# Two heads' keys and values on alternating partitions, in a one-token decode layer

## The chip, the cores and the metric

The kernel runs on one core of one Trainium2 chip. Its time is the device time of one execution in microseconds (us); the metric is the median of several executions. The profile is one further execution, recorded by the hardware profiler. The engines are named as in the profile: PE (TensorE, matrix products), PEld (its weight loads), DVE (VectorE), ACT (ScalarE), POOL (GpSimd) and SP (SyncE, which here only issues transfers). PSUM is the memory that matrix products write.

## The reference

One token `x` of 1024 numbers passes a layer norm. The result goes two ways, and both come back to `x`:

```
xn  = layernorm(x)                                  # 1 x 1024
q   = xn @ wq                                       # 32 heads of 128
k,v = the last 4096 rows of the cache, 4 key heads  # query head h uses key head h // 8
p   = softmax(q k^T / sqrt(128));  o = p v
out = x + o @ wo + (gelu(xn @ w_gate) * (xn @ w_up)) @ w_down
```

All of it is float32. The layer reads wq and wo (16.78 MB each), 4 heads of keys and 4 of values (2.10 MB each, 16.78 MB in all), and w_gate, w_up and w_down (14.68 MB each): 94.38 MB, each byte once, for a product with one row.

## The kernel before, in words

Everything that is read passes through one buffer, `ring`, of 128 partitions with 32768 numbers each. The table `PLAN` (L39) names the loads in order, the column at which each is put, and the older load whose place it takes. `load` (L105) issues a load's transfers on SP's queue, which works in order: SP stops at a transfer until the last reader of that part of the ring has finished, and everything later waits behind it. The order is wq in two halves (`q` 0 and 1), the keys and values of heads 0 and 1 (`k` 0, `v` 0), half of w_gate, the keys and values of heads 2 and 3 (`k` 1, `v` 1), the other half of w_gate, then w_up, wo and w_down.

A head's window is 4096 rows of 128 numbers. `window` (L76) gives each of 128 partitions 32 rows in a run, 16 KB. The two heads of a pair lie side by side in the ring, 4096 columns each; `half` (L440) is the column at which the second begins.

Products with one row are split between PE and DVE. `project` (L227) gives the even rows of a load to PE, which writes to `acc`, and the odd rows to DVE, which adds them up by partition in `part` (`add_scaled`, L207). `projected` (L240) then lets PE sum `part` over the partitions, and adds that to `acc`. `contract` (L425) does the same for wo and w_down with `out_p` and `out_part`.

The main loop (L441) walks the plan in the loads' order, and each engine works in program order. For the keys of a pair (L445): `transpose_keys` (L265) turns 32 blocks of 128x128 on PE, four to a PSUM buffer `kt_p` of which there are two, and ACT copies each buffer to `kT`; for the first pair `projected("q")` and `queries` (L243) follow, in which ACT copies q's rows to `q_sb`, PE turns them and DVE puts them into `qz`; then `scores` (L275) multiplies `qz` with `kT` in eight products of 32 rows, 8 of which are the head's queries, DVE takes each row's maximum, and ACT takes the exponential and its sum. The second head's transposes and scores follow. `values` (L291) turns the probabilities `p`, copies them (`pT`), and multiplies with the values in 32 products into `o_p`.

Each of the four head groups g has four row blocks with a maximum and a sum of their own. `maxima`, `factors` and `normalizers` (L319 to L344) bring them to a common maximum and turn the sums into `weight`; `heads` (L346) scales `o_p`, adds the blocks with the matrix `pick` and spreads the result over `oz`, which wo's product uses. These four stand between the loads of w_gate and w_up.

Of the kernel before, what the change touches and what calls it, by code (L numbers as in the profile page):

```python
# [33 lines left out]
SCALE = DH ** -0.5  # L34
GELU_C = math.sqrt(2.0 / math.pi)
# [15 lines left out]
def tile_decode_layer(  # L51
# [24 lines left out]
    def window(cache, g):  # L76
        return cache[0, g, SK - WIN:, :].rearrange("(p j) d -> p j d", p=P)
# [67 lines left out]
    qz = consts.tile([P, HKV, 32], F32, name="qz")  # L145
# [17 lines left out]
    pick = consts.tile([P, 2, 2, REP, 8], F32, name="pick")  # L163
    nc.vector.memset(pick, 0.0)
    for odd in range(2):
        nc.vector.tensor_copy(
            pick[:, odd, odd], same[:, 0, 0:REP].unsqueeze(2).to_broadcast([P, REP, 8])
        )
# [6 lines left out]
    def layer_norm():  # L175
# [20 lines left out]
        nc.scalar.activation(st[:, 4:5], st[:, 3:4], AF.Sqrt)  # L196

# [45 lines left out]
    def queries():  # L243
        q_sb = work.tile([P, 2, NB], F32, name="q_sb", tag="rows")
        nc.scalar.activation(q_sb, acc["q"], AF.Copy)
        q_p = psum.tile([P, 2, 4, 4], F32, name="q_p", tag="tp", bufs=2)
        for b in range(2):
            for hh in range(4):
                nc.tensor.matmul(
                    q_p[:, b, hh, :], q_sb[:, b, hh * P:(hh + 1) * P], ident[:, 0:P:32],  # L250
                    start=True, stop=True,
                )
            nc.vector.tensor_copy(
                qz[:, 2 * b:2 * b + 2, 0:8].rearrange("p s (t h) -> p s t h", t=2),
                q_p[:, b].rearrange("p h (s t) -> p s t h", s=2),
            )


    m = work.tile([P, HKV], F32, name="m")
    negm = work.tile([P, HKV], F32, name="negm")  # L260
    l = work.tile([P, HKV], F32, name="l")
# [53 lines left out]
    top = work.tile([HKV, 4, 32], F32, name="top")  # L315
    weight = work.tile([P, HKV], F32, name="weight")
    sel = same.rearrange("p c h -> p (c h)")

    def maxima():  # L319
        mt_p = small("mt_p")  # L320
        nc.tensor.transpose(mt_p[:HKV, :P], m, ident)
        nc.vector.reduce_max(
            top[:, 0, :], mt_p[:HKV, :P].rearrange("g (c h) -> g h c", c=4), axis=AX.X
# [4 lines left out]
    def factors():  # L328
        mm_p = small("mm_p")
        nc.tensor.transpose(mm_p[:, :HKV], top.rearrange("g c h -> g (c h)"), ident[:HKV, :HKV])  # L330
        d = work.tile([P, HKV], F32, name="d")
        nc.vector.tensor_sub(d, m, mm_p[:, :HKV])
        e = work.tile([P, HKV], F32, name="e")
        nc.scalar.activation(e, d, AF.Exp, scale=SCALE)
        le = work.tile([P, HKV], F32, name="le")
        nc.vector.tensor_mul(le, l, e)
        return e, le

    def normalizers(e, le):
        ls_p = small("ls_p")  # L340
        nc.tensor.matmul(ls_p[:, :HKV], sel, le, start=True, stop=True)
        r = work.tile([P, HKV], F32, name="r")
        nc.vector.reciprocal(r, ls_p[:, :HKV])
        nc.vector.tensor_mul(weight, e, r)  # L344

    def heads():  # L346
        o_sb = work.tile([P, HKV, DH], F32, name="o_sb")
        for g in range(HKV):
            nc.vector.tensor_scalar(
                o_sb[:, g, :], o_p[:, g, :], weight[:, g:g + 1], None, op0=ALU.mult  # L350
            )
# [3 lines left out]
        for odd in range(2):  # L355
            nc.tensor.matmul(
                ot_p, pick[:, odd].rearrange("p o h s -> p (o h s)"),
                o_sb.rearrange("p (a o) d -> p o a d", o=2)[:, odd],
                start=odd == 0, stop=odd == 1,
            )  # L360
# [80 lines left out]
    for key, _, _ in PLAN:  # L441
# [68 lines left out]
```

## Time and profile before

| | |
|---|---|
| time, median of 3 runs | 229.37 us (229.12 to 229.40) |
| the profiled execution's own time | 229.1 us |
| its span, first to last instruction | 227.3 us |
| busy share of the span: PE, DVE, ACT | 53%, 43%, 15% |
| mean rate of the transfers | 416 GB/s |
| transfers' queue q1 | 3752 packets, 94.38 MB |

The span is what the profile's times count from. The busy shares are means over stages that differ: while keys and values are worked on, PE and ACT do most, and while the weights are, PE and DVE. A packet is what one of the 16 DMA engines moves at a time. The profile gives a queue's packet time as a share of 16 engines over the stretch asked for; packets that overlap on an engine can make that more than 100%. The granted clock is the share of TensorE's 2.4 GHz that it was given in a stretch; 0.50 is the level of 1.2 GHz.

### The profile page before, as it was taken

Reading aid. Unit: us, or ns where it says so; the run is one execution under the profiler, and the core shown is the slowest. Engines: PE = TensorE matmul, PEld = TensorE weight load, DVE = VectorE, ACT = ScalarE, POOL = GpSimd, SP = SyncE. Lnnn points to the kernel's source line nnn. Section 1 sums busy time; section 2 is a strip of 40 time slices with the busy share of each in tenths; the row PEclk is TensorE's granted clock in tenths of the full one; section 3 lists DMA queues with packets and bytes.
Section 4 is the critical chain, followed back from the end, with each engine's and each line's share of the span. In section 5 each row is a group of like instructions: output and inputs, shape, how many; then the busy total and the mean of one; then the engine's idle time right before and its main releaser. Section 6 shows DMA issues by size and latency. Waiting matters only on the chain.

```text
span 227.3 us, 2496 instructions
## 1 busy us (share of the span) xinstructions
PE 120.4 (53%) x1100; PEld 62.9 (28%) x1100; DVE 97.0 (43%) x105; ACT 33.1 (15%) x57; POOL 0.7 (0%) x6
## 2 busy tenths in 40 slices
PE   0120900687866888595745390255219906452754
PEld 0010200154453746364511010111004903121322
DVE  7030920690202091201149489158219606993600
ACT  2000000054174307453200310000000000000000
POOL 1000000000000000000000000000000000000000
PEclk9999975599679699978879978559956655875879
DMA  9899899799999799999999999999999999999991
GB/s 369 370 461 462 369 484 438 334 438 421 437 484 484 327 424 417 421 510 428 394 407 434 439 469 454 394 493 392 430 461 392 438 412 415 421 456 395 424 385 51
DMA packets 3774, 94.53 MB, mean 416 GB/s; under 512 B 426, under 2 KB 434, under 8 KB 1076
## 3 DMA queue, kind: packets, MB, share of 16 engines
q1 hardware_dynamic: 3752, 94.38, 97.0%
q8 instruction: 8, 0.13, 0.2%
q14 instruction: 2, 0.02, 0.0%
q10 hardware_dynamic: 12, 0.01, 0.0%
HBM read 94.38 MB, written 0.00 MB: 415 GB/s over the span
## 4 chain that ended last, share of the span: by engine, by line
DMA 79%; DVE 14%; PE 5%; issue 0%; SPq 0%; DVEq 0%
DMA ring<-in_B_w_gate 26%; DMA ring<-in_A_wq 18%; DMA ring<-in_A_wo 14%; DVE part L212 13%; DMA ring<-in_B_w_up 11%; DMA ring<-in_B_w_down 10%; PE out_p L421 5%; DVE part L210 1%; SPq L118 0%; DVE y L485 0%; DVEq L212 0%
## 5 line engine op out<-in xcount | busy, mean ns | idle before, releaser
L212 DVE SCALAR_TENSOR_TENSOR part<-ring,xz,part 128x3584 f32<-128x3584 f32 (+1 forms) x9 | 37.2, 4129 | 22.2 <-DMA ring<-in_A_wq 12.4
L271 PE MATMUL kt_p<-ident,ring 128*128 128x128 f32 x128 | 21.5, 327 | 7.0 <-ACT kT L272 6.3
L272 ACT ACTIVATE kT<-kt_p 128x512 f32<-128x512 f32 x32 | 17.8, 595 | 43.9 <-PE kt_p L271 43.9
L222 PE MATMUL acc_q<-ring,xz 128*32 128x512 f32 x64 | 11.1, 858 | 22.2 <-DMA ring<-in_A_wq 22.2
L212 DVE SCALAR_TENSOR_TENSOR out_part<-ring,oz,out_part 128x1024 f32<-128x1024 f32 x15 | 19.3, 1285 | 7.9 <-DMA ring<-in_A_wo 7.4
L421 PE MATMUL out_p<-ring,hz 128*32 128x256 f32 x160 | 14.5, 520 | 13.7 <-DMA ring<-in_B_w_down 13.7
L421 PE MATMUL out_p<-ring,oz 128*32 128x256 f32 x128 | 12.3, 569 | 17.0 <-DMA ring<-in_A_wo 17.0
L271 PEld LDWEIGHTS kt_p<-ident,ring 128*128 128x128 f32 x128 | 16.4, 163 | 15.2 <-ACT kT L272 9.6
L222 PE MATMUL acc_u<-ring,xz 128*32 128x512 f32 x56 | 10.8, 838 | 10.7 <-DMA ring<-in_B_w_up 7.0
L283 DVE TENSOR_REDUCE m<-s_p 128x1 f32<-128x1024 f32 x4 | 4.9, 1224 | 26.7 <-PE s_p L280 26.7
L210 DVE TENSOR_SCALAR part<-ring,xz 128x3584 f32<-128x3584 f32 (+1 forms) x3 | 6.5, 2172 | 14.8 <-DMA ring<-in_A_wq 7.4
L421 PEld LDWEIGHTS out_p<-ring,hz 128*32 128x32 f32 x160 | 6.7, 146 | 21.5 <-DMA ring<-in_B_w_down 12.3
L421 PEld LDWEIGHTS out_p<-ring,oz 128*32 128x32 f32 x128 | 5.5, 162 | 23.9 <-DMA ring<-in_A_wo 18.0
L308 PE MATMUL o_p<-ring,pT 128*32 128x128 f32 x256 | 9.5, 309 | 4.7 <-ACT pT L303 4.7
L212 DVE SCALAR_TENSOR_TENSOR out_part<-ring,hz,out_part 128x1024 f32<-128x1024 f32 x8 | 10.3, 1285 | 3.9 <-DMA ring<-in_B_w_down 3.6
L222 PE MATMUL acc_g<-ring,xz 128*32 128x512 f32 x56 | 8.9, 719 | 4.5 <-DMA ring<-in_B_w_gate 4.5
L222 PEld LDWEIGHTS acc_q<-ring,xz 128*32 128x32 f32 x64 | 2.6, 150 | 29.8 <-issue 15.8
L308 PEld LDWEIGHTS o_p<-ring,pT 128*32 128x32 f32 x256 | 8.0, 123 | 5.8 <-ACT pT L303 5.8
L280 PE MATMUL s_p<-kT,qz 128*32 128x512 f32 x64 | 8.4, 645 | 0.0
L222 PEld LDWEIGHTS acc_u<-ring,xz 128*32 128x32 f32 x56 | 2.1, 138 | 17.6 <-DMA ring<-in_B_w_up 7.7
L178 PE MATMUL xt_p<-ident,x_rows 2*128 2x2 f32 x4 | 0.6, 252 | 10.4 <-DMA x_rows<-in_A_x 10.4
L300 PE MATMUL pt_p<-ident,p 128*128 128x128 f32 x32 | 5.9, 347 | 0.0
(94 smaller groups left out, 76.8 us busy)
## 6 DMA issues: line engine op xcount, KB each, us to landing
ring<-in_B_w_gate SPq DMA_DIRECT2D x2, 7168.0 KB
ring<-in_A_k_cache SPq DMA_DIRECT2D x4, 2048.0 KB
ring<-in_A_v_cache SPq DMA_DIRECT2D x4, 2048.0 KB, 23.3
ring<-in_B_w_down SPq DMA_DIRECT2D x2, 4096.0 KB, 24.3
ring<-in_B_w_up SPq DMA_DIRECT2D x2, 3584.0 KB, 26.3
ring<-in_B_w_up SPq DMA_DIRECT2D x1, 7168.0 KB
ring<-in_B_w_down SPq DMA_DIRECT2D x2, 2048.0 KB, 23.8
ring<-in_B_w_down SPq DMA_DIRECT2D x3, 512.0 KB
```

Of the source, the lines that this page charges most:

```text
L178: nc.tensor.transpose(xt_p[:, r * NJ:(r + 1) * NJ], x_rows[:, r:NR * P:NR], ident[:NJ, :NJ])
L210: nc.vector.tensor_scalar(total, w, factor, None, op0=ALU.mult)
L212: nc.vector.scalar_tensor_tensor(total, w, factor, total, op0=ALU.mult, op1=ALU.add)
L222: nc.tensor.matmul(acc[kind][32 * c:32 * c + 32, b, :], z, w[:, n * NB:(n + 1) * NB], start=start, stop=stop,)
L271: nc.tensor.transpose(t_p[:, jj * P:(jj + 1) * P], kn[:, j * DH:(j + 1) * DH], ident)
L272: nc.scalar.activation(kT[:, i, :], t_p, AF.Copy)
L280: nc.tensor.matmul(s_p[32 * c:32 * c + 32, b, :], qz[:, g, :], kT[:, i, :], start=True, stop=True)
L283: nc.vector.reduce_max(m[:, g:g + 1], s_p, axis=AX.XY)
L300: nc.tensor.transpose(t_p[:, jj * P:(jj + 1) * P], p[:, b, jj * P:(jj + 1) * P], ident)
L308: nc.tensor.matmul(o_p[32 * c:32 * c + 32, g, :], pT[:, b, jj, 32 * c:32 * c + 32], vn[:, j * DH:(j + 1) * DH], start=(b == 0 and jj == 0) ...
L421: nc.tensor.matmul(out_p[32 * c:32 * c + 32, :], z, w[:, c * CO:(c + 1) * CO], start=start, stop=stop)
```

## The change

Two heads of a pair now share the ring's columns. `window` cuts a head into 64 runs of 64 rows, 32 KB each, and `load` writes the first head to the even and the second to the odd partitions, 8192 columns wide. So each half of the load holds half of both heads, and each of `transpose_keys`, `scores` and `values` works on half the rows of two heads at a time. `qz` carries both heads' queries, 16 of 32 rows, in one tile for each pair. In the scores every second column belongs to the other head; the maximum is taken for even and odd columns apart, `away` (0 or -1e30, by the row's head) rules one of them out, and the exponential of each is taken with a bias of its own. Two groups now hold two parts of the same heads, so the later steps join them by pairs.

Besides, `projected("q")` and the copy of q's rows come ahead of the first key transposes. A small exponential in the layer norm loads ACT's table there. DVE copies three (1, 4 and 6) of the eight buffers of transposed keys.

```diff
     def window(cache, g):
-        return cache[0, g, SK - WIN:, :].rearrange("(p j) d -> p j d", p=P)
+        return cache[0, g, SK - WIN:, :].rearrange("(p j) d -> p j d", p=P // 2)
...
+        if key[0] in "kv":
+            for odd, src in enumerate(sources(*key)):
+                dst = ring[odd:P:2, at:at + RING // 4]
+                nc.sync.dma_start(dst, src.rearrange("p j d -> p (j d)"))
+            loaded[key] = ring[:, at:at + RING // 4]
+            return
...
-    qz = consts.tile([P, HKV, 32], F32, name="qz")
+    qz = consts.tile([P, 2, 32], F32, name="qz")
...
+    away = consts.tile([P, 2], F32, name="away")
+    nc.vector.reduce_sum(away[:, 1:2], same[:, 0, REP:2 * REP], axis=AX.X)
+    nc.vector.tensor_scalar(away[:, 0:1], away[:, 1:2], -FAR, None, op0=ALU.mult)
+    nc.vector.tensor_scalar(away[:, 1:2], away[:, 1:2], FAR, -FAR, op0=ALU.mult, op1=ALU.add)
...
+        zero = work.tile([P, 1], F32, name="zero")
+        nc.scalar.activation(zero, unit[:, 1:2], AF.Exp)
...
-    def queries():
+    def query_rows():
         q_sb = work.tile([P, 2, NB], F32, name="q_sb", tag="rows")
         nc.scalar.activation(q_sb, acc["q"], AF.Copy)
+        return q_sb
+
+    def queries(q_sb):
...
-            nc.scalar.activation(kT[:, i, :], t_p, AF.Copy)
+            if i in (1, 4, 6):
+                nc.vector.tensor_copy(kT[:, i, :], t_p)
+            else:
+                nc.scalar.activation(kT[:, i, :], t_p, AF.Copy)
...
-                s_p[32 * c:32 * c + 32, b, :], qz[:, g, :], kT[:, i, :], start=True, stop=True
+                s_p[32 * c:32 * c + 32, b, :], qz[:, g // 2, :], kT[:, i, :], start=True, stop=True
             )
-        nc.vector.reduce_max(m[:, g:g + 1], s_p, axis=AX.XY)
-        nc.vector.tensor_scalar(negm[:, g:g + 1], m[:, g:g + 1], -SCALE, None, op0=ALU.mult)
+        s = s_p.rearrange("p b (n odd) -> p odd (b n)", odd=2)
+        m2 = work.tile([P, 2], F32, name="m2")
+        nc.vector.reduce_max(m2, s, axis=AX.X)
+        nc.vector.tensor_add(m2, m2, away)
+        nc.vector.reduce_max(m[:, g:g + 1], m2, axis=AX.X)
+        nc.vector.scalar_tensor_tensor(
+            bias[:, g, :], m[:, g:g + 1].to_broadcast([P, 2]), -SCALE, away, op0=ALU.mult, op1=ALU.add
+        )
         p = work.tile([P, 2, NB], F32, name="p", bufs=2)
-        nc.scalar.activation(
-            p, s_p, AF.Exp, bias=negm[:, g:g + 1], scale=SCALE, accum_out=l[:, g:g + 1]
-        )
+        for odd in range(2):
+            nc.scalar.activation(
+                p.rearrange("p b (n odd) -> p odd (b n)", odd=2)[:, odd], s[:, odd], AF.Exp,
+                bias=bias[:, g, odd:odd + 1], scale=SCALE, accum_out=l[:, g, odd:odd + 1],
+            )
...
     def heads():
...
-        for odd in range(2):
-            nc.tensor.matmul(
-                ot_p, pick[:, odd].rearrange("p o h s -> p (o h s)"),
-                o_sb.rearrange("p (a o) d -> p o a d", o=2)[:, odd],
-                start=odd == 0, stop=odd == 1,
-            )
+        nc.tensor.matmul(ot_p, pick.rearrange("p h s -> p (h s)"), o_sb, start=True, stop=True)
...
             kn = loaded.pop(key)
+            if i == 0:
+                projected("q", 8)
+                q_sb = query_rows()
             transpose_keys(2 * i, kn[:, :half])
             if i == 0:
-                projected("q", 8)
-                queries()
+                queries(q_sb)
```

Left out above: the maxima, factors and normalizers, which gain one reduce, one addition and broadcast operands, the head scaling (two multiplications and two multiply-adds for four multiplications), and the setup of `pick`.

PE's order around the first keys, before: the products with wq, then the first group of key transposes (`kt_p`), and only then the sum of DVE's part (`acc_q<-part`) and q's transposes (`q_p`).

```order
L222 MATMUL acc_q<-ring,xz 32x512 x32
L271 MATMUL kt_p<-ident,ring 128x128 x32
L222 MATMUL acc_q<-part,unit 32x512 x8
L249 MATMUL q_p<-ident,q_sb 128x4 x8
L280 MATMUL s_p<-kT,qz 32x512 x8
L271 MATMUL kt_p<-ident,ring 128x128 x32
```

The same place now:

```order
L235 MATMUL acc_q<-ring,xz 32x512 x32
L235 MATMUL acc_q<-part,unit 32x512 x8
L289 MATMUL kt_p<-ident,ring 128x128 x32
L265 MATMUL q_p<-ident,q_sb 128x4 x8
L301 MATMUL s_p<-kT,qz 32x512 x8
L289 MATMUL kt_p<-ident,ring 128x128 x32
```

The sum has moved ahead of the 32 transposes; the counts of products are the same.

SP's order with its waits, before, from the first keys to w_gate's second half (a name with _49 is a semaphore of that engine or DMA queue):

```order
L118 DMA ring<-in_A_k_cache 128x4096 [waits DMAHW1_49,PE_49]
L118 DMA ring<-in_A_k_cache 128x4096 [waits DMAHW0_49,DVE_49]
L118 DMA ring<-in_A_v_cache 128x4096 [waits PE_49]
L118 DMA ring<-in_A_v_cache 128x4096 [waits DMAHW2_49,DVE_49]
L118 DMA ring<-in_B_w_gate 128x14336 [waits DMAHW3_49,DMAHW6_49,DVE_49,PE_49]
L118 DMA ring<-in_A_k_cache 128x4096 [waits DMAHW7_49,DMAHW4_49,PE_49]
L118 DMA ring<-in_A_k_cache 128x4096 [waits DMAHW5_49,DMAHW0_49,PE_49]
L118 DMA ring<-in_A_v_cache 128x4096 [waits DMAHW1_49,PE_49]
L118 DMA ring<-in_A_v_cache 128x4096 [waits DMAHW2_49,PE_49]
L118 DMA ring<-in_B_w_gate 128x14336 [waits DMAHW3_49,DVE_49,PE_49]
```

The same loads now:

```order
L113 DMA ring<-in_A_k_cache 64x8192 [waits DMAHW1_49,DVE_49,PE_49]
L113 DMA ring<-in_A_k_cache 64x8192 [waits DMAHW0_49]
L113 DMA ring<-in_A_v_cache 64x8192 [waits DVE_49,PE_49]
L113 DMA ring<-in_A_v_cache 64x8192 [waits DMAHW2_49]
L125 DMA ring<-in_B_w_gate 128x14336 [waits DMAHW3_49,DMAHW6_49,DVE_49,PE_49]
L113 DMA ring<-in_A_k_cache 64x8192 [waits DMAHW7_49,DMAHW4_49,PE_49]
L113 DMA ring<-in_A_k_cache 64x8192 [waits DMAHW5_49,DMAHW0_49]
L113 DMA ring<-in_A_v_cache 64x8192 [waits DMAHW1_49,PE_49]
L113 DMA ring<-in_A_v_cache 64x8192 [waits DMAHW2_49]
L125 DMA ring<-in_B_w_gate 128x14336 [waits DMAHW3_49,DVE_49,PE_49]
```

The number of loads and their order are the same. The first load of each pair now carries the waits of both for PE and DVE, and the second follows it at once.

## Rows read from the trace of the kernel before

**Rows 1.** The page: the span, q1's share of 16 engines, the last chain's shares.
```profile
span 227.3 us, 2496 instructions
...
q1 hardware_dynamic: 3752, 94.38, 97.0%
...
DMA 79%; DVE 14%; PE 5%; issue 0%; SPq 0%; DVEq 0%
```

**Rows 2.** Windows: start:end length, busy us of each engine, PEclk, DMA share, GB/s.
```profile
0.00:2.00 2.00, 0.00 (x0) 0.00 (x0) 1.00 (x5) 0.00 (x0) 0.70 (x6) 1.00 0.89 296
...
97.70:223.00 125.30, 66.12 (x649) 32.50 (x652) 63.77 (x59) 8.22 (x15) 0.00 (x0) 0.73 0.99 423
223.00:227.30 4.30, 1.31 (x19) 0.38 (x8) 0.42 (x1) 0.00 (x0) 0.00 (x0) 1.00 0.01 3
```

**Rows 3.** Timeline from 215 us: start, busy, engine, line, operation, count [idle before].
```profile
218.53 5.78 PE L421 MATMUL out_p<-ring,hz 128*32 128x256 f32 x64 [2.54 <-DMA ring<-in_B_w_down]
```

**Rows 4.** DMA queue, 43 to 60 us: packets, MB, share of 16 engines.
```profile
q1 hardware_dynamic: 493, 7.29, 100.5%
```

**Rows 5.** The same, 80 to 97 us.
```profile
q1 hardware_dynamic: 491, 7.26, 100.8%
```

**Rows 6.** The same, 189 to 206 us.
```profile
q1 hardware_dynamic: 240, 7.34, 100.4%
```

**Rows 7.** Timeline of SP: start, time from first to last issue, transfers.
```profile
0.74 0.86 SPq L118 DMA_DIRECT2D ring<-in_A_wq  x2
...
28.86 1.05 SPq L118 DMA_DIRECT2D ring<-in_A_v_cache  x2
...
52.07 17.53 SPq L118 DMA_DIRECT2D ring<-in_A_k_cache  x2
77.24 4.10 SPq L118 DMA_DIRECT2D ring<-in_A_v_cache  x2
...
98.76 26.12 SPq L118 DMA_DIRECT2D ring<-in_B_w_up  x3
```

**Rows 8.** Timeline of PE, the first and second pair of heads.
```profile
41.89 5.04 PE L222 MATMUL acc_q<-ring,xz 128*32 128x512 f32 x32 [13.09 <-DMA ring<-in_A_wq]
46.86 1.09 PE L271 MATMUL kt_p<-ident,ring 128*128 128x128 f32 x8
...
51.97 1.92 PE L222 MATMUL acc_q<-part,unit 128*32 128x512 f32 x16
55.03 1.05 PE L249 MATMUL q_p<-ident,q_sb 128*128 128x4 f32 x8 [1.14 <-ACT q_sb L245]
...
57.34 2.63 PE L280 MATMUL s_p<-kT,qz 128*32 128x512 f32 x16
...
85.00 1.06 PE L271 MATMUL kt_p<-ident,ring 128*128 128x128 f32 x8 [0.63 <-DMA ring<-in_A_k_cache]
...
111.82 0.27 PE L321 MATMUL mt_p<-ident,m 128*4 128x128 f32 x1
```

**Rows 9.** Timeline of DVE: the last row of wq, w_gate's second half.
```profile
46.46 4.49 DVE L212 SCALAR_TENSOR_TENSOR part<-ring,xz,part 128x4096 f32<-128x4096 f32 x1
...
116.55 7.94 DVE L212 SCALAR_TENSOR_TENSOR part<-ring,xz,part 128x3584 f32<-128x3584 f32 x2 [3.77 <-DMA ring<-in_B_w_gate]
```

**Rows 10.** Groups by line: count | busy us, mean ns | idle before, releasers.
```profile
L283 DVE TENSOR_REDUCE m<-s_p 128x1 f32<-128x1024 f32 x4 | 4.9, 1224 | 26.7 <-PE s_p L280 26.7
...
L286 ACT ACTIVATE p<-s_p,negm 128x1024 f32<-128x1024 f32 x4 | 4.5, 1115 | 8.5 <-DVE negm L284 8.5
...
L286 ACT ACT_TABLE_LOAD x1 | 1.3, 1283 | 6.5 <-DVE negm L284 6.5
...
L245 ACT ACTIVATE q_sb<-acc_q 128x1024 f32<-128x1024 f32 x1 | 1.0, 1024 | 1.3 <-PE acc_q L222 1.3
...
L284 DVE TENSOR_SCALAR negm<-m 128x1 f32<-128x1 f32 x4 | 0.6, 153 | 0.1
```

**Rows 11.** Windows, the first two us after PE resumes with wq.
```profile
43.00:45.00 2.00, 2.00 (x12) 0.39 (x8) 2.00 (x1) 0.00 (x0) 0.00 (x0) 0.56 1.09 467
```

More of the change, by code (lines that the diff above doesn't have):

```diff
@@ L34 @@
 SCALE = DH ** -0.5
+FAR = 1e30
 GELU_C = math.sqrt(2.0 / math.pi)
@@ L160, in tile_decode_layer @@
         nc.vector.tensor_copy(same[:, c, :], same[:, 2, :])
-    pick = consts.tile([P, 2, 2, REP, 8], F32, name="pick")
-    nc.vector.memset(pick, 0.0)
-    for odd in range(2):
-        nc.vector.tensor_copy(
-            pick[:, odd, odd], same[:, 0, 0:REP].unsqueeze(2).to_broadcast([P, REP, 8])
-        )
+    pick = consts.tile([P, 2 * REP, 8], F32, name="pick")
+    nc.vector.tensor_copy(pick, same[:, 0, 0:2 * REP].unsqueeze(2).to_broadcast([P, 2 * REP, 8]))
     low = consts.tile([P, 8], F32, name="low")
     nc.vector.reduce_sum(low, ident.rearrange("p (h s) -> p s h", s=8), axis=AX.X)
+    away = consts.tile([P, 2], F32, name="away")
+    nc.vector.reduce_sum(away[:, 1:2], same[:, 0, REP:2 * REP], axis=AX.X)
+    nc.vector.tensor_scalar(away[:, 0:1], away[:, 1:2], -FAR, None, op0=ALU.mult)
+    nc.vector.tensor_scalar(away[:, 1:2], away[:, 1:2], FAR, -FAR, op0=ALU.mult, op1=ALU.add)
     def small(name):
@@ L253, in queries @@
             nc.vector.tensor_copy(
-                qz[:, 2 * b:2 * b + 2, 0:8].rearrange("p s (t h) -> p s t h", t=2),
+                qz[:, b, 0:16].rearrange("p (s t h) -> p s t h", s=2, t=2),
                 q_p[:, b].rearrange("p h (s t) -> p s t h", s=2),
@@ L259, in tile_decode_layer @@
     m = work.tile([P, HKV], F32, name="m")
-    negm = work.tile([P, HKV], F32, name="negm")
-    l = work.tile([P, HKV], F32, name="l")
+    bias = work.tile([P, HKV, 2], F32, name="bias")
+    l = work.tile([P, HKV, 2], F32, name="l")
     keys, probs = {}, {}
@@ L312, in values @@
                     )
-    top = work.tile([HKV, 4, 32], F32, name="top")
-    weight = work.tile([P, HKV], F32, name="weight")
+    top = work.tile([2, 4, 32], F32, name="top")
+    weight = work.tile([P, 2, 2], F32, name="weight")
     sel = same.rearrange("p c h -> p (c h)")
@@ L320, in maxima @@
         mt_p = small("mt_p")
-        nc.tensor.transpose(mt_p[:HKV, :P], m, ident)
+        for f in range(2):
+            nc.tensor.transpose(mt_p[:2, f * P:(f + 1) * P], m[:, f:HKV:2], ident)
         nc.vector.reduce_max(
-            top[:, 0, :], mt_p[:HKV, :P].rearrange("g (c h) -> g h c", c=4), axis=AX.X
+            top[:, 0, :], mt_p[:2, :2 * P].rearrange("g (c h) -> g h c", c=8), axis=AX.X
         )
@@ L329, in factors @@
         mm_p = small("mm_p")
[L330 to L333, printed above, removed]
+        nc.tensor.transpose(mm_p[:, :2], top.rearrange("g c h -> g (c h)"), ident[:2, :2])
+        d = work.tile([P, 2, 2], F32, name="d")
+        nc.vector.tensor_sub(
+            d, m.rearrange("p (g f) -> p g f", f=2), mm_p[:, :2].unsqueeze(2).to_broadcast([P, 2, 2])
+        )
+        e = work.tile([P, 2, 2], F32, name="e")
         nc.scalar.activation(e, d, AF.Exp, scale=SCALE)
         le = work.tile([P, HKV], F32, name="le")
-        nc.vector.tensor_mul(le, l, e)
+        nc.vector.tensor_add(le, l[:, :, 0], l[:, :, 1])
+        nc.vector.tensor_mul(le, le, e.rearrange("p g f -> p (g f)"))
         return e, le
@@ L341, in normalizers @@
         nc.tensor.matmul(ls_p[:, :HKV], sel, le, start=True, stop=True)
-        r = work.tile([P, HKV], F32, name="r")
-        nc.vector.reciprocal(r, ls_p[:, :HKV])
-        nc.vector.tensor_mul(weight, e, r)
+        r = work.tile([P, 2], F32, name="r")
+        nc.vector.reduce_sum(r, ls_p[:, :HKV].rearrange("p (g f) -> p g f", f=2), axis=AX.X)
+        nc.vector.reciprocal(r, r)
+        nc.vector.tensor_mul(weight, e, r.unsqueeze(2).to_broadcast([P, 2, 2]))
     def heads():
-        o_sb = work.tile([P, HKV, DH], F32, name="o_sb")
-        for g in range(HKV):
+        o_sb = work.tile([P, 2, DH], F32, name="o_sb")
+        for g in range(2):
             nc.vector.tensor_scalar(
-                o_sb[:, g, :], o_p[:, g, :], weight[:, g:g + 1], None, op0=ALU.mult
+                o_sb[:, g, :], o_p[:, 2 * g, :], weight[:, g, 0:1], None, op0=ALU.mult
+            )
+            nc.vector.scalar_tensor_tensor(
+                o_sb[:, g, :], o_p[:, 2 * g + 1, :], weight[:, g, 1:2], o_sb[:, g, :],
+                op0=ALU.mult, op1=ALU.add,
             )
         ot_p = psum.tile([P, 2, DH], F32, name="ot_p", tag="tp", bufs=2)
-        for odd in range(2):
-            nc.tensor.matmul(
-                ot_p, pick[:, odd].rearrange("p o h s -> p (o h s)"),
-                o_sb.rearrange("p (a o) d -> p o a d", o=2)[:, odd],
-                start=odd == 0, stop=odd == 1,
-            )
+        nc.tensor.matmul(ot_p, pick.rearrange("p h s -> p (h s)"), o_sb, start=True, stop=True)
         own = work.tile([P, 2, 8, WIDE], F32, name="own", tag="rows")
```

## The prediction

> **What bounds the kernel now.** I read the page's totals first [rows 1]. The queue that carries the weights and the cache (q1) is busy for 97.0% of the span with 94.38 MB, and the chain that ended last is 79% DMA, 14% DVE and 5% PE. The windows then say where the missing 3% is [rows 2]: between 97.7 and 223.0 us the DMA engines are busy 0.99 of the time, and after 223.0 nothing moves. So there is one uninterrupted stream from about 1 us to 223 us, and a tail: the last matmuls run to 224.3 us (218.53 + 5.78) [rows 3], then come one addition and the output. A change gains only what shortens that stream or that tail, and it loses whatever opens a hole in the stream. The tail is not touched.
>
> Next I read how the stream runs on the rows to be changed. In 43 to 60 us, inside the first keys and values, q1 has 493 packets, 7.29 MB, 100.5% of 16 engines [rows 4]; in 80 to 97 us, inside the second pair, 491 packets, 7.26 MB and 100.8% [rows 5]; in 189 to 206 us, inside w_down, whose first two loads bring 32 KB a partition, 240 packets, 7.34 MB and 100.4% [rows 6]. The first two are the layout of before (16 KB a partition), the third is the packet size that the change gives to keys and values.
>
> Last I read when SP can issue. Its waits don't hurt as long as each load is issued before the loads ahead of it have drained. The second pair's keys go out from 52.07 to 69.60 (52.07 + 17.53) and its values from 77.24 to 81.34 [rows 7].
>
> **The change part by part.**
>
> *Larger packets.* Engine time for each MB is share times 16 engines times 17 us over MB: 1.005 x 272 / 7.29 = 37.50 us [rows 4], 1.008 x 272 / 7.26 = 37.77 us [rows 5], and 1.004 x 272 / 7.34 = 37.21 us [rows 6]. Keys and values are 8 transfers of 2.10 MB, 16.78 MB. The mean of the first two less the third is 0.43 us, times 16.78 over 16 engines: 0.45 us of stream. By the rates of the same windows (MB over 17 us: 429 and 427 against 432 GB/s) it is 16.78/0.428 - 16.78/0.432 = 39.2 - 38.8 = 0.4 us. Lower end: none, if what slows these windows goes by bytes or by other traffic. Shares above 100% say that packets overlap a little, which hides part of a packet's fixed cost, so I take 0.35 us.
>
> *64 rows on every second partition.* No row shows a transfer that names 64 partitions. Below, it costs nothing, if the 16 engines share these rows as evenly as the 128. Above, if pairs of engines meet on one path, it takes twice the time, 39.2 us more. The nearest rows, rows 4 to 6, show all engines full with three different row counts, so I take zero and keep the other as a rival. The Trainium skill (SBUF — State Buffer, "Door 1: The DMA port swizzle") speaks against transfers to 64 partitions: neighbouring ones reach half of the 16 ports, and it gives 196 GB/s for them; by that rate the 16.78 MB would take 86 us, not 39. By the same section's formula every second partition from 0 to 126 reaches all 16 ports, which leaves the sum as it is; no row here shows either.
>
> *Waits of SP.* Before, each half of a load waited for the half of the ring that it overwrites; now both of a pair wait for the whole. For the first pair that costs nothing: before, the last of them was issued by 29.9 us [rows 7], and PE waits for wq's second half until 41.89 [rows 8]. For the second pair I work out when PE has done with the first.
> - Keys of pair 0: the first half is in use from 46.86 [rows 8], and the second is 2.10 MB / 0.430 = 4.9 us behind it, so all has landed by 51.8 us. PE now idles from 46.9 to 51.0, when DVE ends the last row of wq (46.46 + 4.49) [rows 9], and then sums q in 1.92 us. After the long wait before 41.89 PE ran at a granted clock of 0.56 in 43 to 45 us, so near 1.2 of 2.4 GHz [rows 11]; if the short one has the same effect the sum takes up to 3.8 us. Transposes start at 52.9 to 54.8 us.
> - Eight groups of transposes, with ACT's copies between them, took 46.86 to 51.97, 5.1 us, 0.64 for a group. DVE now copies three of eight. The trace has no such copy; DVE's 128x1024 reduce out of PSUM took 1.22 us [rows 10], so about 0.6 us for half as many elements: no faster than ACT. What two copiers gain lies between nothing and the waits between pairs of groups; the copy of q's rows, 1.02 us on ACT [rows 10], now stands ahead of the first of them and costs about as much. I leave 5.2 us.
> - q's transposes (55.03 to 57.34, 2.3 us) and the scores (2.63 us) follow [rows 8]: the first scores end at 63.0 to 64.9 us, where before they ended at 59.97.
> - From there to the issue of the second values it took 81.34 - 59.97 = 21.4 us. Off it goes the table load, 1.28 us [rows 10], which now stands in the layer norm, where ACT has little else. To it come, for each of two groups of scores, three small DVE steps in place of one at 0.15 us (0.3 us and the gaps, 0.45) and a second exponential: two of 512 elements for one of 1024 at 1.115 us add between nothing and 0.56 us [rows 10], I take 0.3. In all 21.4 - 1.3 + 1.5 = 21.6 us. The operands now take every second element; the lower end is no cost, and if it doubled the reduce (1.22 us) and the exponentials (1.1 us) they would cost 2 x 2.3 = 4.6 us more. I take none.
> - So the second values are issued by 84.6 to 86.5 us, 3 to 5 us later than now. They are needed when the second keys have drained. PE waited for the first half of these until 85.00, the other half is 2.10 / 0.428 = 4.9 us behind, so all have landed by 89.9, and the last packet is a little earlier: 87 to 89 us. From issue to first packets it takes at most 1.3 us: issued at 0.74 [rows 7], with 296 GB/s already in the window that ends at 2.0 [rows 2]. The limit is 86 to 87.5 us. I take no hole, but the cover is thin.
> - Queued behind these values on SP are w_gate's second half and all later loads, in order. The second keys now go out together when the second group of transposes ends, about 73 us where the later one went at 69.3; they are needed when w_gate's first half has drained, 4.19 MB (9.8 us) ahead of the second keys' end and so at 77 to 79 us, less the lead: near 76.
> - Pair 1: PE starts at 89.9 rather than 85.00 and needs about the 26.8 us it took to 111.8, so until 116.7. Behind that stands DVE's reduce of the maxima, and behind that, in order, DVE's work on w_gate, which began at 116.55 [rows 9]. The last w_up load waits for it (issued by 98.76 + 26.12 = 124.9 [rows 7]); 55.6 MB stand ahead of it, of which 0.6 has moved at 2.0 us, and at 430 GB/s it is needed at about 129. A slip of 3 us is covered.
>
> *The rest.* The constants lose a memset and gain three small DVE operations while wq's first half is still on its way. The factors, normalizers and heads gain and lose a few short operations while w_up streams, 14.68 MB or 34 us. Cost: zero, since no load waits on them with less than the slack above; without that cover, some three steps of 0.15 us, about 0.5 us.
>
> **The sum.** 229.1 us (span 227.3 [rows 1] and 1.8 around it) less 0.35 is 228.75 for an execution like the profiled one. That one lay 0.27 below the median of the runs shown; the same 0.35 off 229.37 gives 229.0 us.
>
> **The rivals.**
> *Late values.* A hole in front of the second values. For it: an issue at 84.6 to 86.5 against a limit of 86 to 87.5, and the two unknowns (clock, strided operands) both push one way. Against it: every other estimate in that chain is from rows at both clock levels. It decides from the moment the issue passes the limit, and each us beyond is a us of the stream. With the low clock and half of the doubled operands it is 86.5 + 2.3 = 88.8 against 86.7, the middle of the limit: 229.0 + 2.1 = 231.1 us; with all of the 4.6 us 233.4 us, with none of it 229.0. That is slower than before.
> *Two engines on one path.* Keys and values at half the rate: 229.4 + 39.2 = 268.6 us; if engines fall out of step, half of it, 249. For it: 64 rows is a count that no row shows. Against it: every second partition still spreads over the whole range, and the trace's rates don't fall for any row count seen.
> *The packets do not matter.* The engine cuts or overlaps so that the 0.35 us does not appear: 229.4 us, no change. For it: the stretch from 97.7 to 223.0 us moves 423 GB/s [rows 2], below either window of keys and values, with packets of many sizes in it, so other things than packet size set the rate too.
>
> **How the numbers follow.** The likeliest case, a slightly shorter stream with no hole, has 64%; its own range is 228.3 to 229.4. Its lower part would need fewer stray stalls as well as fewer packets. Late values have 17%, the shared path 7%, no effect of packets 12%. A difference under 0.2%, 0.46 us, is about what a measurement of this kernel cannot tell from no change. 0.35 us is under that: of the 64, 28 lie beyond it and 36 within. Faster 0.28; same 0.36 + 0.12 = 0.48; slower 0.17 + 0.07 = 0.24. The range reaches from 228.3 to 231.0: it leaves out the shared path and the longer half of the holes, and some 3% below.
>
> **What would show it.** In the changed profile the windows inside keys and values should hold half as many large packets at about 432 GB/s, with engine time near 37.2 us for each MB; the second values should be issued near 85 us with no window of low DMA share at 86 to 90 us; the table load should stand before 20 us; the last matmuls should end some 0.3 us earlier. A DMA share well under 0.9 in a window between 85 and 92 us, or keys and values that move at 215 to 300 GB/s, would make the prediction wrong; so would a tail after the last packet that is not the 4.3 us of before [rows 2].

## The result, and the profile after

The changed kernel takes 230.50 us (median of 22 runs, 228.56 to 232.35), the kernel before 229.22 in the same job (22 runs, 228.94 to 229.40). The ratio is 1.0036, interval [1.0019, 1.0053]: a little slower, where 229.0 us was forecast. The comparison leaves out the four longest runs of the changed kernel (over 232 us), and one of experiment e7 below (232.51), so these ratios are nearer to one than those of the medians. What stands out is the spread, 3.8 us where the kernel before has 0.5: some runs are faster than any of before, most are slower.

The profiled execution took 231.73 us. On its page (span, q1's share of 16 engines, the last chain) the stream is as long in bytes and less full than in [rows 1]:

```profile
span 229.9 us, 2512 instructions
...
q1 hardware_dynamic: 3240, 94.38, 96.2%
...
DMA 53%; PE 24%; DVE 15%; ACT 5%; issue 1%; SPq 0%; ACTq 0%; DVEq 0%
```

A quarter of the chain that ended last is now PE. The timeline of SP (start, time to the last issue, transfers) answers to [rows 7]:

```profile
74.57 1.11 SPq L113 DMA_DIRECT2D ring<-in_A_k_cache  x2
87.35 1.11 SPq L113 DMA_DIRECT2D ring<-in_A_v_cache  x2
90.76 0.33 SPq L125 DMA_DIRECT2D ring<-in_B_w_gate  x1
103.99 23.42 SPq L125 DMA_DIRECT2D ring<-in_B_w_up  x3
145.18 0.33 SPq L125 DMA_DIRECT2D ring<-in_A_wo  x1
```

The second pair's values go out at 87.35, 10 us after the first of them did before and 6 us after the last. The windows (columns as in [rows 2]) show what follows:

```profile
51.00:53.00 2.00, 1.88 (x12) 0.57 (x16) 0.06 (x1) 0.00 (x0) 0.00 (x0) 0.50 0.87 377
53.00:55.00 2.00, 2.00 (x14) 0.34 (x7) 0.00 (x0) 0.17 (x1) 0.00 (x0) 0.50 1.21 524
55.00:57.00 2.00, 2.00 (x11) 1.77 (x10) 0.30 (x1) 1.44 (x2) 0.00 (x0) 0.51 0.81 336
63.00:65.00 2.00, 2.00 (x15) 0.70 (x18) 0.17 (x1) 0.00 (x0) 0.00 (x0) 0.69 0.93 401
87.00:91.00 4.00, 3.90 (x42) 1.22 (x34) 0.00 (x0) 0.00 (x0) 0.00 (x0) 1.00 0.84 283
88.00:90.00 2.00, 2.00 (x21) 0.61 (x17) 0.00 (x0) 0.00 (x0) 0.00 (x0) 1.00 0.97 270
223.00:225.00 2.00, 2.00 (x31) 0.90 (x23) 0.00 (x0) 0.00 (x0) 0.00 (x0) 0.70 0.53 207
```

From 87 to 91 us 283 GB/s flow, where the same stretch of before had 414: 131 x 4 us = 0.52 MB short, 1.2 us of a stream of 430 GB/s. That is the hole. Part of it is its end: from 88 to 90 us the engines count as 0.97 busy and move only 270 GB/s. The 1.2 us depend on what they are compared with: against e7 below, which has the same layout, no hole and 451 GB/s in this window, it is 1.6 us. In the queue's own windows (43 to 60 us, then 80 to 97) the first pair answers to [rows 4] and the second to [rows 5]:

```profile
q1 hardware_dynamic: 271, 7.31, 99.8%
...
q1 hardware_dynamic: 253, 6.72, 96.2%
```

The first pair is what was forecast: half the large packets, engine time 0.998 x 272 / 7.31 = 37.1 us for each MB (forecast 37.2, before 37.50). Rows on 64 partitions cost nothing. The Trainium skill (SBUF — State Buffer, "Door 1: The DMA port swizzle") gives half the rate in the limit for transfers to the 64 partitions 0 to 63; these, on every second partition, lose none (431 GB/s in 43 to 60 us, before 430), as its formula has it. The second pair moved 0.54 MB less in its window. PE's timeline shows why it was late ([rows 8] of before):

```profile
51.12 3.64 PE L235 MATMUL acc_q<-part,unit 128*32 128x512 f32 x16 [3.17 <-DVE part L225]
54.69 6.10 PE L289 MATMUL kt_p<-ident,ring 128*128 128x128 f32 x32
...
63.22 3.16 PE L301 MATMUL s_p<-kT,qz 128*32 128x512 f32 x16
...
85.33 1.96 PE L337 MATMUL o_p<-ring,pT 128*32 128x128 f32 x64 [0.31 <-ACT pT L332]
...
152.64 5.24 PE L235 MATMUL acc_u<-ring,xz 128*32 128x512 f32 x28 [4.97 <-DMA ring<-in_B_w_up]
...
220.57 6.34 PE L454 MATMUL out_p<-ring,hz 128*32 128x256 f32 x64 [2.55 <-DMA ring<-in_B_w_down]
```

PE waits 3.17 us for DVE's last row of wq, then runs at a granted clock of 0.50 for 6 us (the windows from 51 to 57): the sum takes 3.64 us. The first scores end at 66.38, before at 59.97, and the last values' product at 87.29, six hundredths ahead of the issue. Two products that wait for a load mark how late the stream is: w_up's 152.64 against this line of before,

```profile
150.56 5.32 PE L222 MATMUL acc_u<-ring,xz 128*32 128x512 f32 x28 [6.97 <-DMA ring<-in_B_w_up]
```

so 2.08 us, and w_down's last 220.57 against 218.53 [rows 3], 2.04. All of it was lost ahead of 150 us. It is more than the 1.2 us of the window from 87 to 91; why the loads land later than the bytes of the hole account for stays open. The last matmuls themselves took 6.34 us for 5.78, which makes the 2.6 us of the span. The clock does not explain that: it was 0.70 in 223 to 225 us, and two us earlier in the kernel before, in 221 to 223 us, 0.69. Transfers still moved 20 GB/s in 225 to 227 us, where before 4 GB/s were left in 223 to 225.

DVE, which began w_gate's second half at 116.55 [rows 9], now does so at 119.11, right behind the maxima. PE's line shows that this load landed only at about 118.68, so most of this delay is the hole again:

```profile
118.68 3.63 PE L235 MATMUL acc_g<-ring,xz 128*32 128x512 f32 x28 [0.32 <-DMA ring<-in_B_w_gate]
...
118.39 0.41 DVE L352 TENSOR_REDUCE top<-mt_p 2x32 f32<-2x256 f32 x1 [9.31 <-PE mt_p L351]
...
119.11 7.92 DVE L225 SCALAR_TENSOR_TENSOR part<-ring,xz,part 128x3584 f32<-128x3584 f32 x2
```

The groups by line (count | busy us, mean ns | idle before) answer to [rows 10]; ACT's table load of 1.28 us now stands at 14.20:

```profile
L291 DVE COPY kT<-kt_p 128x512 f32<-128x512 f32 x12 | 8.3, 692 | 24.5 <-PE kt_p L289 24.5
...
L293 ACT ACTIVATE kT<-kt_p 128x512 f32<-128x512 f32 x20 | 11.7, 597 | 14.9 <-PE kt_p L289 14.9
...
L306 DVE TENSOR_REDUCE m<-s_p 128x2 f32<-128x1024 f32 x4 | 4.9, 1225 | 8.4 <-PE s_p L301 8.4
L314 ACT ACTIVATE p<-s_p,bias 128x512 f32<-128x512 f32 x8 | 5.6, 710 | 16.7 <-DVE bias L309 16.7
```

The reduce over every second element costs what the plain one did (1225 against 1224 ns); two exponentials of 710 for one of 1115 add 0.3 us.

### The profile page after: what moved, and what is told of

It is laid out like the page before. It is cut to its first block, busy times and chain, and to the rows that moved or that the text cites. A ratio compares the mean times of both kernels' runs of the same rounds, so it can differ in the third digit from the quotient of the medians.

```text
span 229.9 us, 2512 instructions
## 1 busy us (share of the span) xinstructions
PE 123.1 (54%) x1099; PEld 62.1 (27%) x1099; DVE 106.8 (46%) x128; ACT 28.1 (12%) x54; POOL 0.7 (0%) x6
## 4 chain that ended last, share of the span: by engine, by line
DMA 53%; PE 24%; DVE 15%; ACT 5%; issue 1%; SPq 0%; ACTq 0%; DVEq 0%
DMA ring<-in_A_wq 18%; DMA ring<-in_A_wo 13%; DMA ring<-in_B_w_up 11%; DVE part L225 11%; DMA ring<-in_B_w_down 10%; PE kt_p L289 6%; PE out_p L454 5%; PE o_p L337 5%; PE s_p L301 4%; DVE m L306 2%; ACT p L314 2%; ACT kT L293 2%; PE acc_q L235 2%; PE acc_g L235 2%; ACT pT L332 1%
## 5 line engine op out<-in xcount | busy, mean ns | idle before, releaser
L225 DVE SCALAR_TENSOR_TENSOR part<-ring,xz,part 128x3584 f32<-128x3584 f32 (+1 forms) x9 | 37.1, 4127 | 16.4 <-DMA ring<-in_A_wq 12.4
L291 DVE COPY kT<-kt_p 128x512 f32<-128x512 f32 x12 | 8.3, 692 | 24.5 <-PE kt_p L289 24.5
L337 PE MATMUL o_p<-ring,pT 128*32 128x128 f32 x256 | 10.6, 334 | 6.6 <-ACT pT L332 6.6
L293 ACT ACTIVATE kT<-kt_p 128x512 f32<-128x512 f32 x20 | 11.7, 597 | 14.9 <-PE kt_p L289 14.9
L337 PEld LDWEIGHTS o_p<-ring,pT 128*32 128x32 f32 x256 | 9.1, 134 | 7.6 <-ACT pT L332 7.6
L301 PE MATMUL s_p<-kT,qz 128*32 128x512 f32 x64 | 8.9, 680 | 0.0
L306 DVE TENSOR_REDUCE m<-s_p 128x2 f32<-128x1024 f32 x4 | 4.9, 1225 | 8.4 <-PE s_p L301 8.4
L314 ACT ACTIVATE p<-s_p,bias 128x512 f32<-128x512 f32 x8 | 5.6, 710 | 16.7 <-DVE bias L309 16.7
L235 PE MATMUL acc_g<-ring,xz 128*32 128x512 f32 x56 | 7.2, 595 | 0.3 <-DMA ring<-in_B_w_gate 0.3
```

The lines of the kernel that those rows point to most:

```text
L225: nc.vector.scalar_tensor_tensor(total, w, factor, total, op0=ALU.mult, op1=ALU.add)
L235: nc.tensor.matmul(acc[kind][32 * c:32 * c + 32, b, :], z, w[:, n * NB:(n + 1) * NB], start=start, stop=stop,)
L291: nc.vector.tensor_copy(kT[:, i, :], t_p)
L301: nc.tensor.matmul(s_p[32 * c:32 * c + 32, b, :], qz[:, g // 2, :], kT[:, i, :], start=True, stop=True)
L306: nc.vector.reduce_max(m2, s, axis=AX.X)
L314: nc.scalar.activation(p.rearrange("p b (n odd) -> p odd (b n)", odd=2)[:, odd], s[:, odd], AF.Exp, bias=bias[:, g, odd:odd + 1], scale=SC ...
```

## The experiments

The theory: the hole in front of the second pair's values is the whole loss; it comes from both transfers waiting for the second group's products, and from a first pair that is done some 6 us later. The rivals: the layout itself costs (64 rows, strided operands), or the later sum costs without any hole. The time before was 229.25 in the first job, 229.19 in the second, 229.22 in the last. "Issue" is when SP issues the second pair's values, and "w_up" is when PE starts on the last load of w_up, for which it waits (150.56 before); both are from the profiled execution.

| | issue, us | w_up, us | time (runs), us | ratio, interval |
|---|---|---|---|---|
| changed kernel | 87.35 | 152.64 | 230.50 (22) | 1.0036 [1.0019, 1.0053] |
| e1 values in halves | 83.08 to 87.47 | 150.29 | 229.06 (12) | 0.9999 [0.9985, 1.0012] |
| e2 PE takes three rows | 84.41 | 150.03 | 229.81 (12) | 1.0025 [1.0009, 1.0042] |
| e3 order alone | 83.74 to 87.96 | 150.72 | 229.27 (11) | 1.0001 [0.9992, 1.0010] |
| e4 layout alone | 90.25 | 155.11 | 234.32 (4) | 1.0219 [1.0204, 1.0234] |
| e5 ACT copies all | 88.32 | 153.26 | 230.38 (10) | 1.0057 [1.0036, 1.0079] |
| e6 sum after | 87.57 | 152.54 | 230.94 (4) | 1.0077 [1.0049, 1.0105] |
| e7 PE rows, late maxima | 82.86 | 150.37 | 229.03 (12) | 0.9996 [0.9979, 1.0013] |
| e8 joint wait, old layout | 85.18 | 150.62 | 230.49 (12) | 1.0043 [1.0020, 1.0065] |
| e9 e1, e2 and e7 together | 82.23 to 87.11 | 150.30 | 229.09 (12) | 1.0002 [0.9990, 1.0015] |
| e10 late table | 88.11 | 153.54 | 230.73 (6) | 1.0076 [1.0051, 1.0101] |

**e1: values in halves.** The changed kernel, but each head's second values as two column halves, so that the first half waits for the first group only.

```diff
-            for odd, src in enumerate(sources(*key)):
-                dst = ring[odd:P:2, at:at + RING // 4]
-                nc.sync.dma_start(dst, src.rearrange("p j d -> p (j d)"))
+            cuts = 2 if key == ("v", 1) else 1
+            n = RING // 4 // cuts
+            for cut in range(cuts):
+                for odd, src in enumerate(sources(*key)):
+                    dst = ring[odd:P:2, at + cut * n:at + (cut + 1) * n]
...
```

> The changed kernel with one thing different: the second pair's values are loaded by columns, in two halves for each head (four transfers of 64 rows of 16 KB), so that the first half waits for the first group's values only. Theory late values: the hole in the stream before these transfers comes from their waiting for both groups (issued at 87.35 us in the changed kernel). The first half should go out near 84 us, the window 80 to 97 us should be back at about 428 GB/s, and the time should be 229.0 us (228.6 to 229.4) with a small spread. Theory slow transfers: transfers to every second partition, or of 32 KB packets, are slower in themselves; the time stays at 230 to 231 with a wide spread.

The windows of its profile at the place of the hole:

```profile
87.00:89.00 2.00, 2.00 (x22) 0.69 (x17) 0.00 (x0) 0.00 (x0) 0.00 (x0) 1.00 0.96 410
89.00:91.00 2.00, 1.75 (x15) 0.87 (x9) 0.15 (x1) 0.60 (x1) 0.00 (x0) 1.00 1.00 426
```

No hole, and the time of before: the median is 1.4 us lower from the split alone, with the layout, the order and the strided operands left in. Two of the twelve runs are still late (230.04 and 230.68 us), so the small spread that was expected did not come. The split also brings 16 KB packets back for these four transfers; that is not what closes the hole, since e2 and e7 keep 32 KB and have none. So the transfers of the layout cost nothing in themselves; what they wait for does.

**e2: PE takes three rows.** PE takes three of the four rows of wq's second half, so that it does not idle ahead of the sum.

```diff
-            if r % 2 == 0:
+            if r % 2 == 0 or (kind == "q" and jj == 1 and r == 3):
```

> The changed kernel, but PE takes three of the four rows of wq's second half, and DVE one, so that q's sum need not wait for DVE until 51.1 us. The layout and the waits are as changed. Late values: PE works through from 42 to about 50 us and sums q at the high clock (1.9 in place of 3.6 us); the key transposes start near 52 in place of 54.7, the second values go out near 85, there is no hole, and the time is that of larger packets alone, 228.8 us (228.5 to 229.2). Slow transfers: 230 to 231.

PE's and then DVE's timeline:

```profile
49.67 1.89 PE L235 MATMUL acc_q<-part,unit 128*32 128x512 f32 x16
...
118.93 0.41 DVE L352 TENSOR_REDUCE top<-mt_p 2x32 f32<-2x256 f32 x1 [9.34 <-PE mt_p L351]
...
119.64 7.92 DVE L225 SCALAR_TENSOR_TENSOR part<-ring,xz,part 128x3584 f32<-128x3584 f32 x2
```

The same 16 products take 1.89 us, the issue comes 2.9 us earlier, the hole at 87 us is gone (516 GB/s in 87 to 89). Of the time 0.56 us of 1.28 stays, which is neither of the two expectations. Of the span (median 227.6 us, changed kernel 228.7, before 227.5) almost nothing stays: four of the twelve runs are longer by 0.5 to 1.6 us outside their span, which nothing here explains. What is late in the profiled execution is wo. PE's lines of e2, and then the line of before, for the last load of w_up and the first of wo:

```profile
150.03 4.96 PE L235 MATMUL acc_u<-ring,xz 128*32 128x512 f32 x28 [1.81 <-DMA ring<-in_B_w_up]
...
170.66 6.59 PE L454 MATMUL out_p<-ring,oz 128*32 128x256 f32 x64 [10.74 <-DMA ring<-in_A_wo]
```

```profile
169.92 5.88 PE L421 MATMUL out_p<-ring,oz 128*32 128x256 f32 x64 [9.47 <-DMA ring<-in_A_wo]
```

From the one to the other it takes 20.63 us, before 19.36 (from 150.56): 1.27 us are lost here. DVE, behind the maxima, starts w_gate at 119.64, and wo, which waits for DVE's later rows, is issued at 145.72, where before it was 140.75. This is the second late point. In the changed kernel it costs nothing (19.34 us, 152.64 to 171.98), because the hole has already made the stream later.

**e3: order alone.** The kernel before with the sum and the copy of q's rows ahead of the key transposes, nothing else of the change.

> The kernel before with one part of the change alone: q's sum and the copy of q's rows stand ahead of the first key transposes. Late values by the layout's waits: the first group's values end some 6 us later than before, near 83 us, and the second's near 87, but each half of the second pair's values waits for its own half only, so there is no hole: 229.2 us (229.0 to 229.5), same as before. Rival, the order of the sum opens the hole by itself: 230 us or more.

The sum takes 3.26 us, the first scores end at 66.4, the first of the two values' transfers goes at 83.74 and the second at 87.96: as late a pair as in the changed kernel, and no loss. What differs is that the first transfer still waits for the first group only.

**e4: layout alone.** The changed kernel with the sum after the transposes, no early table and all copies on ACT.

```diff
-        zero = work.tile([P, 1], F32, name="zero")
-        nc.scalar.activation(zero, unit[:, 1:2], AF.Exp)
...
-            if i in (1, 4, 6):
-                nc.vector.tensor_copy(kT[:, i, :], t_p)
-            else:
-                nc.scalar.activation(kT[:, i, :], t_p, AF.Copy)
+            nc.scalar.activation(kT[:, i, :], t_p, AF.Copy)
...
```

> The changed kernel with only the layout: q's sum stands after the first key transposes again, the exponential's table is loaded where it is first used, and ACT copies all eight buffers of keys. Late values by the layout's waits: PE waits for all keys of the first pair until about 51.8 us, and the values of the second pair go out at 86 to 88 us; a hole of 0 to 2 us, 229.3 to 231 us. Rival, the order of the sum is the cause: no hole, 228.9 us.

Its first transposes on PE, and two windows:

```profile
52.00 4.66 PE L286 MATMUL kt_p<-ident,ring 128*128 128x128 f32 x24 [4.38 <-DMA ring<-in_A_k_cache]
```

```profile
89.00:91.00 2.00, 2.00 (x56) 1.40 (x52) 0.00 (x0) 0.00 (x0) 0.00 (x0) 1.00 0.11 41
91.00:97.00 6.00, 5.55 (x47) 2.90 (x37) 0.00 (x0) 2.25 (x5) 0.00 (x0) 1.00 0.96 350
```

PE's line for the last load of w_up:

```profile
155.11 5.24 PE L232 MATMUL acc_u<-ring,xz 128*32 128x512 f32 x28 [3.14 <-DMA ring<-in_B_w_up]
```

It is 5 us slower, more than either expectation. A first group now needs rows of both transfers, so PE starts the keys at 52.00 and not at 46.86 [rows 8]. That is 5.1 of the 8.9 us by which the issue, at 90.25, is later than that of the last values before (81.34); 41 GB/s flow in 89 to 91. So the layout's waits alone make the hole, and the other three parts of the change give back 3.8 us together. The prediction had priced the table at 1.28 us and the copies at nothing.

**e5, e6, e10: one part undone each.** In e5 ACT copies all eight buffers, in e6 the sum stands after the transposes, in e10 the early exponential is missing (three of the edits of e4, one at a time).

> The changed kernel with ACT copying all eight buffers of transposed keys, the other parts kept. My prediction held that the DVE copies gain about what the moved copy of q's rows costs, nothing. The run with the layout alone (234.3 us) says that the three other parts together give back 3.8 us. If the copies are most of that, since DVE can copy while ACT takes the exponentials, the second values go out near 89 us and the time is 231.5 to 232.5; if they are nothing, 230.5 as changed.

> The changed kernel with q's sum after the first key transposes again, the other parts kept. PE waits for all keys of the first pair until about 52 us either way; the sum then runs at the high clock (1.9 us in place of 3.6) but q's copy stands behind it with nothing beside it. If the order of the sum is what gives time back, 231.5 us or more; if the low clock takes away what the order gives, 230.5 us as changed (229.5 to 231).

> The changed kernel without the early exponential, so ACT's table is loaded at the first exponential of the scores, as before. Theory (each us of the chain in front of the second values is a us of the hole): the table load of 1.28 us stands between the first scores' maxima and the first exponential again, the second values are issued at 88.5 to 89 us where the changed kernel issued them at 87.35, the windows at 87 to 91 us show one more us without transfers, and the median is 231.3 to 231.9 us, ratio 1.009 to 1.012. Rival (PE, not ACT, sets the pace behind the first scores, since it still turns the second half of the keys): the table is hidden behind PE's transposes, the issue stays at 87 to 87.6 us and the median at 230.3 to 230.7.

e10's table load on ACT and its window at the hole:

```profile
67.86 1.28 ACT L312 ACT_TABLE_LOAD   x1 [7.35 <-DVE bias L307]
```

```profile
87.00:91.00 4.00, 4.00 (x68) 1.73 (x59) 0.00 (x0) 0.00 (x0) 0.00 (x0) 1.00 0.58 152
```

PE's line for the last load of w_up:

```profile
153.54 5.77 PE L233 MATMUL acc_u<-ring,xz 128*32 128x512 f32 x28 [4.54 <-DMA ring<-in_B_w_up]
```

From the end of the first scores to the issue it takes 22.2 us (65.88 to 88.11), in the changed kernel 21.0 (66.38 to 87.35): the 1.28 us of the load are on the path, not hidden behind PE. These are single executions, and the stretch varies: it is 20.2 us in e2 and in e6, which differ from the changed kernel only ahead of it. The hole is (414 - 152) x 4 / 430 = 2.4 us. Issue and time, 88.11 and 230.73, lie between the two expectations, and the interval overlaps that of the changed kernel, as do those of e5 and e6. So the three parts are shown together (3.8 us). In one execution each, the issue comes 1.0 us later without DVE's copies (0.4 of it is there when the sum starts, 51.49 for 51.12), 0.8 without the early table and 0.2 with the sum after; the time of each alone is not settled.

**e8: joint wait in the old layout.** e3, with the second pair's values issued in the opposite order, so that both wait for the second group; layout and packets are those of before.

```diff
+        if key == ("v", 1):
+            n = RING // 8
+            for g in (1, 0):
+                dst = ring[:, at + g * n:at + (g + 1) * n]
+                nc.sync.dma_start(dst, sources(*key)[g].rearrange("p j d -> p (j d)"))
...
```

> The kernel before, layout and packets as before, with q's sum ahead of the key transposes (which alone gave 229.27 us, no difference) and the second pair's values loaded in the opposite order, so that both transfers wait for the second group's values and none goes out ahead. Late values: with the sum ahead these end at 87.9 us, and the first transfer that used to go out at 83.7 now goes out then: the stream gets a hole of 0.7 to 1.7 us near 88 us, 230 to 231 us, with a spread like that of the changed kernel. If the layout's transfers are the cause, 229.3 us, as with the order alone.

The median is 230.49, that of the changed kernel. The twelve runs stand in two groups, five at 229.01 to 229.32 and seven at 230.38 to 231.32. The profiled one is of the first, with the issue at 85.18 and 434 GB/s in 87 to 89 us, so the hole of the others was not seen in a trace. The time shows that joint wait and late pair are enough, since e8 differs from e3 in the wait alone; the layout isn't needed.

**e7 and e9: a version that beats both?** e7 is e2 with the maxima's steps moved behind DVE's rows of w_gate; e9 adds e1's halves.

```diff
-            if i == 1:
-                maxima()
...
+                maxima()
```

> The kernel with PE on three rows of wq's second half, and besides it the maxima's transpose and reduce behind DVE's rows of w_gate's second half instead of ahead of them. In the run with three rows alone, 229.8 us, DVE began these rows at 119.6 us, after the maxima, where the kernel before began at 116.6, and the first load of wo went out at 145.7 us, some 5 us later than before and about when w_up had drained. If late second values and this second late load are all that holds the layout back, there is no hole left, wo goes out near 142.5 us, and the time is that of larger packets: 228.8 us (228.6 to 229.1), spread under 0.6 us. If something else slows the stream, 229.5 or more.

> The changed kernel with three edits together: PE takes three of the four rows of wq's second half, the maxima stand behind w_gate's rows, and the second pair's values are loaded in two column halves for each head. Theory (the changed kernel loses only what its two late points cost, and gains some 0.4 us from fewer packets): with both points taken away every run lies at 228.5 to 229.0 us, median near 228.75, ratio to before 0.998; the values' first half is issued before 83 us, w_up's last load is not late, and no window between 85 and 92 us has a DMA share under 0.9. Rival (the packets give nothing, or the smaller transfers and the low clock take it back): median 229.1 to 229.3, ratio 0.9995 to 1.0005, with no hole either.

In e7 DVE starts w_gate at 116.39, wo is issued at 143.43, and from the last load of w_up to the first of wo it takes 19.36 us again. PE's waits in e7, and then in e9, the last of them against 218.53 [rows 3]:

```profile
150.37 5.71 PE L235 MATMUL acc_u<-ring,xz 128*32 128x512 f32 x28 [4.44 <-DMA ring<-in_B_w_up]
...
218.32 5.72 PE L454 MATMUL out_p<-ring,hz 128*32 128x256 f32 x64 [2.56 <-DMA ring<-in_B_w_down]
```

```profile
218.38 2.37 PE L459 MATMUL out_p<-ring,hz 128*32 128x256 f32 x40 [0.94 <-DMA ring<-in_B_w_down]
```

They are 0.21 and 0.15 us earlier, about what the larger packets are worth: without a hole the wait stands at 218.26 to 218.38 in three executions with the new layout (e1, e7, e9) and at 218.53 to 218.73 in three with the old (before, e3, e8). e7 still has late runs (230.96 at a clock of 0.776, 232.51 at 0.813), so it misses the spread of 0.6 us that was expected. In e9 all twelve spans are 227.1 to 227.3 us (before, in that job, 227.3 to 227.6), whatever the clock. So with both late points the spread of the spans is gone, but the time is no better than before: 229.09, not the expected ratio of 0.998; two runs (229.96, 230.59) are longer outside their span, which nothing here explains. Neither version beats the kernel before by more than can be measured.

## Why the prediction was wrong

The failed step is "I take no hole, but the cover is thin". The mechanism of the rival *Late values* was right, with its place. Both sides of the comparison that ruled it out were mis-sized: the issue, forecast at 84.6 to 86.5 us, came at 87.35, and the limit, forecast at 86 to 87.5, lay near 85.

- *The first scores end at 63.0 to 64.9 us.* They ended at 66.38. The wait for DVE (51.0 forecast, 51.12) and the sum were inside the range, at its slow end (3.64 us of 1.92 to 3.8). The transposes were forecast at 5.2 us and took 6.10, the scores at 2.63 and took 3.16. Part of both ran at the low clock (0.51 in 55 to 57 us, 0.69 in 63 to 65). The prediction gave the low clock to the sum alone and kept the durations of before for all that follows. In e2, where no wait stands ahead of the sum, the transposes take the 5.2 us, but the scores 3.53, at a clock of 0.50 in 61 to 63 us.
- *21.6 us from there to the issue.* 20.97, so 0.6 shorter. The second exponential cost its 0.3 us, the strided operands next to nothing, and the early table gave its 1.28 us by e10.
- *The values are issued by 84.6 to 86.5.* 87.35: 1.5 us later from the first step, 0.6 earlier from the second, on the upper end.
- *The limit is 86 to 87.5.* It lay lower. In the column "w_up" of the table the changed kernel is 2.27 us behind e7, e6 2.17, e5 2.89, e10 3.17 and e4 4.74; each time the issue less this loss is 84.9 to 85.5. e2 and e8's profiled run, issued at 84.41 and 85.18, lose nothing there. So each us of issue past some 85 us was about a us of the stream, as the rival said, and most of the forecast issues lay past it. The prediction's own terms, 87 to 89 less 1.3, begin at 85.7. Even against 86, an issue at 86.5 was a hole already, and *Late values* got 17%.
- *A slip of 3 us is covered.* For the last load of w_up it was: in e2 DVE starts w_gate 3.09 us later than before, that load is issued by 127.95 (needed at about 129), and w_up is on time. The prediction did not price wo, which waits for DVE's next rows: there e2 loses 1.27 us, and e7, with the maxima moved, none. In time the gain from e2 to e7 rests on medians whose intervals overlap.
- *Larger packets, 0.35 us.* Right in sign, with 0.15 to 0.47 us between the executions without a hole. In time it is not shown: e9 has 1.0002 [0.9990, 1.0015], so *The packets do not matter* is not refuted there. Seven of the 22 runs took 228.56 to 229.51 us, at clocks of 0.804 to 0.813, and nearly all the slower ones stand at 0.771 to 0.799. This fits that, with no cover left, a run's clock decides whether it has the hole; no trace of a fast run of the changed kernel shows it.
- *DVE's copies are worth nothing net.* For the time e5 agrees (230.38), for the issue they gave up to 1.0 us. A copy takes 692 ns on DVE and 597 on ACT, as forecast.
- *Two engines on one path* did not come. The price of nothing for the 64 rows was right, though rows 4 to 6 could not show it: all of them hold transfers to 128 partitions, not "three different row counts". The tail after the last matmul stayed (2.99 us to the end of the span, as before).

## What to carry to other kernels

When two transfers that waited one after the other come to wait together, compare the issue with the time at which the queue runs dry, at the slow end of every step in between and at the early end of the limit; cover smaller than what the low clock adds to these steps is no cover. Then do the same for every later load behind the wait, not only for the next one. A loss of this kind looks like noise: read the spread of the runs, not only the median. Split the transfer along the axis in which its readers finish, as e1 did, and the layout costs nothing that the median shows.

## What the runs showed of the hardware

- After an idle time of 3.17 us PE's next 16 products took 3.64 us at a granted clock of 0.50; after 3.92 to 4.14 us of idle time (e10, e1, e3) they took 2.82 to 3.26 us, and with no idle time ahead of them (e2) 1.89 us at a clock of 1.00.
- The queue comes back slowly from a hole. In 88 to 90 us the DMA share is 0.97 at 270 GB/s, which makes 0.97 x 2 x 16 / 0.54 = 57 us of engine time for each MB (an estimate from this row), against 37.1 in the full stream; in e10 it is 0.99 at 246 GB/s in 89 to 91 us. Whether these packets take longer or overlap more is not shown.
- 64 rows on every second partition load at the rate of 128 (431 against 430 GB/s in 43 to 60 us).
